# Half-height matmuls of an attention and GEGLU kernel: natural 128-row operands with one exchange of the array halves per unit, and a first chunk in quarters

## The chip, the cores and the metric

The kernel runs on one core of a Trainium2 chip. The metric is the device time of one execution in microseconds (us), median of several runs: 566.61 us before the change (three runs, 566.18 to 568.24). The engines are TensorE (PE, with its weight loads PEld), VectorE (DVE), ScalarE (ACT), GpSimd (POOL) and SyncE (SP, which only issues DMAs here).

## The reference

Shapes: x is [2048, 448]; 16 query heads and 8 key/value heads of 256; only the last 512 keys are attended to; the MLP is 1792 wide. All is bf16.

```
xn = layernorm(x)                                  # no gain, no bias
q  = xn @ wq                                       # [2048, 16*256]
p  = softmax(q @ k[-512:].T / 16)                  # per head, no mask
s  = (p @ v[-512:]) @ wo                           # [2048, 448]
g  = silu((gelu_tanh(xn @ w_gate) * (xn @ w_up)) @ w_down)
out = x + s * g
```

The contraction of the first products is over 448 = 3*128 + 64, which is what this change is about.

## The kernel before, in words

The program is written as a list of operations (`Plan.op`, L69). Each names its engine and the buffers that it reads and writes; `schedule` (L90) turns the dependences into semaphore waits, and `emit` puts each engine's operations out in program order. No engine reorders its list, so the order in the text is the order of the work. Two operations of PE never wait for each other (L80). DMAs are issued from SP, ACT and POOL, each a queue in order.

The 2048 tokens are 16 tiles of 128 and 4 chunks of 512.

- **Layernorm** (L345 to L358). `ln_stats` computes mean and variance of a tile on DVE and 1/sqrt(variance + eps) in two POOL operations (L348, L350). `ln_norm` writes the normalised rows to `xn` on DVE, each group of 64 columns twice, side by side: 896 columns.
- **Transposing** gives `xnT`, with the 448 columns of xn on partitions as 7 blocks of 64, each held twice (partitions 0 to 63 and 64 to 127). The four tiles of chunk 0 go through PE and PSUM (`ln_tp_pe`, L364, copies by ACT and DVE at L380 and L382), the others by DMA on SP's queue (`ln_tp_dma`, L360).
- **The MLP's first products**. A unit is one block of 128 of the 1792 columns, `gu` (L407). Gate weights lie on partitions 0 to 63 and up weights on 64 to 127, 7 blocks of 64 rows each (`load_w`, L316). `pair` (L395) lists 14 matmuls of 64 rows, alternating between the halves of the array, which work at the same time: gate into one PSUM bank, up into the next. A unit uses 2 of the 8 banks, in a ring of four pairs. `gu_evac` (L421) applies gelu on ACT and multiplies by up on DVE, which frees the banks. There are 4 * 14 = 56 units.
- **Chunk 0** starts in halves of 256 tokens for units 0 to 2 (L441 to L458), among the transposes of its four tiles and warm-up matmuls on zeros (`warm`, L386).
- In the main loop (L474) the statistics and the norm of the tiles 4 to 15 alternate with the units, one step per unit from unit 2 on. `down` (L429) multiplies a finished chunk with w_down and stores silu-like gates in `g2`. The loads of wq, v, k, wo are put out at units 27 and 30, those of w_down (`wd`) and of x at the very beginning, on SP's queue (L336 to L342).
- **Attention** (L574 to L594), for each chunk and each group of 8 heads: the queries by `q_pair` (L508), again half-height pairs, head h in one half of the array and head h+4 in the other; then per head scores and exp (`s_mm`), and probabilities times values (`pv`), with the transposing of the result by DMA; the projection with wo of the previous chunk stands between. The end (L595 on) is wo for the last chunk.

Of the kernel before, what the change touches and what calls it, by code (L numbers as in the profile page):

```python
# [11 lines left out]
P = 128  # L12
# [24 lines left out]
class Plan:  # L37
# [31 lines left out]
    def op(self, eng, fn, reads=(), writes=(), dma=False):  # L69
        o = Op(eng, fn, dma)  # L70
        raw = {b.writer: None for b in reads if b.writer is not None}
        deps = dict(raw)
        for b in writes:
            if b.writer is not None:
                deps[b.writer] = None
            deps.update((x, None) for x in b.readers)


        for d in deps:
            if d.eng == eng and not d.dma and not dma and (eng == "pe" or d not in raw):  # L80
                continue
            o.deps.append(d)
        for b in writes:
            b.writer, b.readers = o, []
        for b in reads:
            b.readers.append(o)
        self.ops.append(o)
        return o
# [75 lines left out]
def bass_recurrent_scan__sliding_block_cached__geglu_ffn__prompt_kernel(  # L164
# [25 lines left out]
    NK = D // R  # L190
    att_scale = float(Dh) ** -0.5
    assert D == NK * R and Dh == 256 and W == 512 and Hq == 2 * Hkv and Hq % 8 == 0
    assert NT == 4 * NQC and NF % 2 == 0 and (NQC * NF) % 4 == 0
# [5 lines left out]
    with es:  # L199
# [19 lines left out]

        ident, a_ident, _ = place("ident", [P, P], BF16)  # L220
        b_ident = K.buf(a_ident, 256)
        nhalf, a, _ = place("nhalf", [P, 1], F32)
        b_nhalf = K.buf(a, 4)
        stats, a, _ = place("stats", [P, NT, 6], F32)
# [10 lines left out]
        xnT, a, _ = place("xnT", [P, NK, S], BF16)  # L235
# [8 lines left out]
        wq, a, _ = place("wq", [P, NK, NG, HG // 2, 2, P], BF16)  # L244
        b_wql = [[K.buf() for i in range(2)] for g in range(NG)]
# [13 lines left out]
        NXN = (rw_end - a2) // (2 * D * 2)  # L259
        xn, a, a2 = place("xn", [P, NXN, NK, 2, R], BF16, at=a2)  # L260
        b_xn = sbuf_bufs(a, 2 * D * 2, NXN)
# [3 lines left out]
        wgu, a, at = place("wgu", [P, NK, F], BF16, at=rf)  # L265
        b_wgu = K.buf(a, at - a)
        FBL = [0, 4, 9, NF]
        b_wl = [[K.buf() for j in range(2)] for i in range(3)]
        wd, a, at = place("wd", [P, NF, D], BF16, at=at)
# [3 lines left out]
        NGL = 3  # L273
# [4 lines left out]
        NEX = 2  # L278
# [25 lines left out]
        def mms(lst, reads, writes):  # L304
# [5 lines left out]
            K.op("pe", fn, reads, writes)  # L310
# [5 lines left out]
        def load_w(q, i, j):  # L316
            w = (B_w_gate, B_w_up)[j]
            lo, hi = FBL[i] * P, FBL[i + 1] * P
            dma(q, wgu[R * j:R * j + R, :, lo:hi], w[:, lo:hi].rearrange("(k p) f -> p k f", p=R), (), (b_wl[i][j],))
# [6 lines left out]
        load_w("act", 0, 1)  # L326
        K.op("pool", lambda e: e.memset(ident[:, :], 0.0), (), (b_ident,))
        K.op("pool", lambda e: e.affine_select(
            out=ident[:, :], in_=ident[:, :], compare_op=ALU.not_equal, fill=1.0, base=0,
            pattern=[[-1, P]], channel_multiplier=1), (b_ident,), (b_ident,))  # L330
        K.op("dve", lambda e: e.memset(nhalf[:, :], -0.5), (), (b_nhalf,))
        K.op("dve", lambda e: e.memset(gl[:, 0, :], 0.0), (), (b_gl[0],))
        K.op("dve", lambda e: e.memset(va[:, :, :, Dh:VW], 1.0), (), (b_va1,))

        act(tmp[:, 1, 0:1], nhalf[:, :], ACT.Gelu_apprx_tanh, (b_nhalf,), (b_tmp[1][0],))
        load_w("sp", 1, 0)  # L336
        load_w("sp", 1, 1)
        load_x("sp", 4, 4)
        load_w("sp", 2, 0)
        load_w("sp", 2, 1)  # L340
        load_x("sp", 8, 8)
        dma("sp", wd[:, :, :], B_w_down.rearrange("(f p) d -> p f d", p=P), (), (b_wd,))  # L342


        def ln_stats(t):  # L345
            K.op("dve", lambda e: e.bn_stats(stats[:, t, :], x4[:, t, :]), (b_x4[t],), (b_stats[t],))  # L346
            K.op("dve", lambda e: e.bn_aggr(mv[:, t, :], stats[:, t, :]), (b_stats[t],), (b_mv[t],))  # L347
            K.op("pool", lambda e: e.tensor_scalar(  # L348
# [3 lines left out]

        def ln_norm(t):
            s = t % NXN
            src = x4[:, t, :].rearrange("p (k r) -> p k r", r=R).unsqueeze(2).broadcast_to([P, NK, 2, R])
            K.op("dve", lambda e: e.tensor_scalar(  # L356
                xn[:, s, :, :, :], src, mv[:, t, 0:1], rstd[:, t:t + 1],
                op0=ALU.subtract, op1=ALU.mult), (b_x4[t], b_mv[t], b_rstd[t]), (b_xn[s],))  # L358

        def ln_tp_dma(t):  # L360
            s = t % NXN
            dma_t(xnT[:, :, t * P:(t + 1) * P], xn[:, s, :, :, :].rearrange("p k u r -> p (k u r)"), (b_xn[s],), (b_xnT[t],))

        def ln_tp_pe(t, split):  # L364
            s = t % NXN
            for eng, b, lo, hi in split:
                tp = bank[b].bitcast(BF16)

                def fn(e, tp=tp, lo=lo, hi=hi):
                    ins = None  # L370
                    for k in range(lo, hi):
                        ins = e.transpose(tp[:, k * P:(k + 1) * P], xn[:, s, k, :, :].rearrange("p u r -> p (u r)"), ident[:, :])  # L372
                    return ins
                K.op("pe", fn, (b_xn[s], b_ident), (b_ps[b],))
            for eng, b, lo, hi in split:
                tp = bank[b].bitcast(BF16)
                o = xnT[:, lo:hi, t * P:(t + 1) * P]
                i = tp[:, lo * P:hi * P].rearrange("p (k c) -> p k c", c=P)
                if eng == "act":
                    act(o, i, ACT.Copy, (b_ps[b],), (b_xnTh[t][lo > 0],))  # L380
                else:
                    K.op("dve", lambda e, o=o, i=i: e.tensor_copy(o, i), (b_ps[b],), (b_xnTh[t][lo > 0],))  # L382

        b_xnTh = [[b_xnT[t], K.buf()] for t in range(NT)]
# [10 lines left out]
        def pair(b, w, x, ks, start, stop, lo=0, hi=QC):  # L395
            return [(bank[b + j][:, lo:hi], w(k)[R * j:R * j + R], x(k)[R * j:R * j + R],
                     start and k == ks[0], stop and k == ks[-1]) for k in ks for j in range(2)]
# [4 lines left out]
        def xr_bufs(c, lo=0, hi=4):  # L402
            return [b for t in range(c * 4 + lo, c * 4 + hi) for b in b_xnTh[t]]

        GUB = (0, 2, 6, 4)

        def gu(n, part=None):  # L407
            c, f = divmod(n, NF)
            wi = [i for i in range(3) if FBL[i] <= f][-1]
            b = GUB[n % 4]  # L410
            w = lambda k: wgu[:, k, f * P:(f + 1) * P]
            if part is None:
                lst = pair(b, w, xs(c), range(NK), True, True)
                xb = xr_bufs(c)
            else:
                lo, hi = part * QC // 2, (part + 1) * QC // 2
                lst = pair(b, w, xs(c, lo, hi), range(NK), part == 0, part == 1, lo, hi)
                xb = xr_bufs(c, 2 * part, 2 * part + 2)
            mms(lst, b_wl[wi] + [b_wgu] + xb, (b_ps[b], b_ps[b + 1]))

        def gu_evac(n):  # L421
            c, f = divmod(n, NF)
            s = n % NGL
            b = GUB[n % 4]
# [15 lines left out]

        warm(14, 3)  # L441
        ln_stats(0)
        ln_stats(1)
        ln_norm(0)
        ln_tp_pe(0, [("act", 6, 0, NK)])
        warm(2, 3)
        ln_norm(1)
        ln_tp_pe(1, [("dve", 4, 0, 4), ("act", 5, 4, NK)])
        warm(3, 3)
        ln_stats(2)  # L450
        ln_stats(3)
        gu(0, 0)
        ln_norm(2)
        ln_tp_pe(2, [("dve", 6, 0, 4), ("act", 7, 4, NK)])
        gu(1, 0)
        ln_norm(3)
        ln_tp_pe(3, [("dve", 4, 0, 4), ("act", 5, 4, NK)])
        gu(2, 0)  # L458
# [8 lines left out]
        def load_wq(g, j):  # L467
            lo = (g * HG + j * HG // 2) * Dh
            hi = lo + HG // 2 * Dh
            dma("pool", wq[R * j:R * j + R, :, g, :, :, :].rearrange("p k h e d -> p k (h e d)"),  # L470
                A_wq[:, lo:hi].rearrange("(k p) f -> p k f", p=R), (), (b_wql[g][j],))

        DOWN_AT = {NF + 1: 0, 2 * NF + 3: 1, 3 * NF + 1: 2}
        for n in range(NQC * NF):  # L474
            if n < 3:
                gu(n, 1)
            else:
                gu(n)
            gu_evac(n)
            t = 4 + (n - 2) // 2  # L480
            if n >= 2 and t < NT:
                if n % 2 == 0:
                    ln_stats(t)
                else:
                    ln_norm(t)
                    ln_tp_dma(t)
            if n == 27:
                for g in range(NG):
                    for j in range(2):
                        load_wq(g, j)  # L490
# [4 lines left out]
            if n == 30:  # L495
# [6 lines left out]
            if n in DOWN_AT:  # L502
                down(DOWN_AT[n], 0)

# [3 lines left out]
        def q_pair(c, g, i, b):  # L508

            h, e = divmod(i, 2)  # L510
            mms(pair(b, lambda k: wq[:, k, g, h, e, :], xs(c), range(NK), True, True),
                b_wql[g] + xr_bufs(c), (b_ps[b], b_ps[b + 1]))
            act(qT[:, h, e, :], bank[b], ACT.Copy, (b_ps[b],), (b_qT[h][e],))
            h2 = h + HG // 2
            K.op("dve", lambda v: v.tensor_copy(qT[:, h2, e, :], bank[b + 1]), (b_ps[b + 1],), (b_qT[h2][e],))  # L515
# [57 lines left out]
        bx, by = 0, 4  # L573
        for c in range(NQC):  # L574
            for g in range(NG):
                for i in range(HG):
# [87 lines left out]
```

The softmax here doesn't subtract the row's maximum and nothing guards it: scores larger than these inputs give would overflow.

## Time and profile before

| | |
|---|---|
| median of three runs | 566.61 us (566.18 to 568.24) |
| profiled execution | 567.22 us, its span 565.4 us |
| PE busy in the span | 553.6 us, 98% |
| weight loads | 310.6 us, 55% |
| DVE, ACT, POOL busy | 284.3 us (50%), 209.3 us (37%), 34.5 us (6%) |
| queries, 896 matmuls of 64 rows | 98.1 us |
| MLP's first products with 512 tokens, 742 recorded | 80.9 us |
| first MLP matmul | at 8.96 us |
| norm of one tile on DVE (896 columns) | 0.739 us |
| DMA moved | 42.03 MB |

The span runs from the first to the last instruction of the program; the profiled execution's own time holds a little more on both sides. Busy time of PE is the union of its matmuls' intervals, and those overlap, so a mean of 376 ns for a matmul of 512 columns does not mean that one starts every 376 ns. In a wait "A <- B: sum, times, longest", A stood idle and B's end let it go on. A line number is that of kernel.py; L308 is the helper through which nearly all matmuls go, so groups are told apart by the tiles that they write and read.

### The profile page before, as it was taken

To read this page: it belongs to the slowest core of one execution; us is meant where nothing else is said; L and a number is where in the kernel's file an instruction comes from. 1 tells how busy PE (TensorE), PEld (TensorE's weight loads), DVE (VectorE), ACT (ScalarE), POOL (GpSimd) and SP (SyncE) were. 2 spreads that over 40 slices of the span, in tenths; PEclk is the share of its full clock that TensorE was granted. 3 is DMA by queue.
4 is the path that set the end of the run, shared out by engine and by line. 5 is a ranking of instruction groups with operands and counts; after the bars stand their busy time and mean duration, and the time that the engine had idled before them with its cause. 6 is when DMAs were issued, how large, how long until landed. Compare 5 with 4: busy or idle time off the path is not lost.

```text
span 565.4 us, 9758 instructions
## 1 busy us (share of the span) xinstructions
PE 553.6 (98%) x4037; PEld 310.6 (55%) x4073; DVE 284.3 (50%) x736; ACT 209.3 (37%) x272; POOL 34.5 (6%) x70
## 2 busy tenths in 40 slices
PE   7989999999999999999999999999999999999997
PEld 5534444444466466455655654566465456656656
DVE  5864734244267367314654661267467224665632
ACT  2422423234354554302536531054553303535500
POOL 2111451000000000000000000000000000000000
PEclk9999999999999999999999999999999999999999
DMA  9961599940014124111340430124125011431421
GB/s 205 271 106 23 90 196 243 294 99 1 0 38 84 30 49 84 20 32 37 76 73 18 76 57 17 33 64 84 21 59 84 9 34 48 77 59 30 74 48 34
DMA packets 101708, 42.03 MB, mean 74 GB/s; under 512 B 90464, under 2 KB 98912, under 8 KB 101664
## 3 DMA queue, kind: packets, MB, share of 16 engines
q1 hardware_dynamic: 97648, 29.45, 27.5%
q0 software_dynamic: 3264, 11.27, 8.1%
q10 hardware_dynamic: 752, 0.69, 0.5%
q8 instruction: 32, 0.52, 0.4%
q14 instruction: 12, 0.10, 0.1%
HBM read 17.92 MB, written 1.84 MB: 35 GB/s over the span
## 4 chain that ended last, share of the span: by engine, by line
PE 93%; DVE 3%; issue 1%; DMA 1%; POOL 1%; ACT 0%; DVEq 0%; ACTq 0%
PE bank L308 93%; DVE actT L426 1%; DVE stats L346 1%; POOL rstd L350 1%; DVE xn L356 1%; DMA xnT<-xn 1%; DMA x_65<-in_A_x_dram 0%; PE bank L372 0%; POOL ve L348 0%; DVE mv L347 0%; DVE xnT L382 0%; DVE g_57 L437 0%; ACT gl L302 0%; ACT tmp L302 0%; PE bank L390 0%
## 5 line engine op out<-in xcount | busy, mean ns | idle before, releaser
L302 ACT ACTIVATE expT<-bank 128x1024 bf16<-128x1024 f32 x128 | 123.7, 1022 | 150.6 <-PE bank L308 150.5
L540 DVE TENSOR_SCALAR onorm<-bank,rden 128x256 bf16<-128x256 f32 x256 | 123.8, 484 | 9.6 <-DVE rden L538 0.5
L308 PE MATMUL bank<-va,expT 128*128 128x257 bf16 x1024 | 124.2, 273 | 0.0
L308 PE MATMUL bank<-qT,kT 128*128 128x512 bf16 x476 | 115.9, 379 | 2.9 <-issue 1.3
L308 PEld LDWEIGHTS bank<-va,expT 128*128 128x128 bf16 x1024 | 99.1, 98 | 27.7 <-DVE onorm L540 1.7
L308 PE MATMUL bank<-xnT,wq 64*128 64x512 bf16 x896 | 98.1, 376 | 0.0
L308 PE MATMUL bank<-wo,oT 128*128 128x448 bf16 (+1 forms) x544 | 97.6, 341 | 0.0
L308 PE MATMUL bank<-xnT,wgu 64*128 64x512 bf16 (+1 forms) x826 | 86.0, 366 | 2.4 <-DMA xnT<-xn 2.1
L308 PEld LDWEIGHTS bank<-qT,kT 128*128 128x128 bf16 x512 | 49.1, 97 | 52.3 <-issue 3.4
L308 PEld LDWEIGHTS bank<-wo,oT 128*128 128x128 bf16 x544 | 53.1, 98 | 44.0
L538 DVE RECIPROCAL rden<-bank 128x1 f32<-128x1 f32 x256 | 40.9, 160 | 67.0 <-PE bank L308 67.0
L308 PEld LDWEIGHTS bank<-xnT,wq 64*128 64x128 bf16 x896 | 43.0, 94 | 52.9 <-issue 1.5
L302 ACT ACTIVATE qT<-bank 128x512 bf16<-128x512 f32 x64 | 38.2, 597 | 80.1 <-PE bank L308 80.1
L515 DVE CAST qT<-bank 128x512 bf16<-128x512 f32 x64 | 44.3, 692 | 45.9 <-PE bank L308 45.9
L308 PEld LDWEIGHTS bank<-xnT,wgu 64*128 64x128 bf16 x826 | 39.8, 94 | 47.9 <-DVE actT L426 2.6
L302 ACT ACTIVATE gl<-bank 128x512 bf16<-128x512 f32 x56 | 33.4, 597 | 52.7 <-PE bank L308 48.1
L426 DVE TENSOR_TENSOR actT<-bank,gl 128x512 bf16<-128x512 f32 x56 | 38.5, 687 | 28.5 <-ACT gl L302 28.1
L563 DVE SCALAR_TENSOR_TENSOR tmp<-bank,g_57 128x448 f32<-128x448 f32 (+1 forms) x17 | 10.2, 597 | 82.5 <-PE bank L308 82.5
L308 PE MATMUL bank<-wd,actT 128*128 128x448 bf16 x224 | 43.1, 353 | 0.0
L308 PEld LDWEIGHTS bank<-wd,actT 128*128 128x128 bf16 x224 | 21.7, 98 | 21.2 <-issue 1.3
L296 POOL DMA_DIRECT2D xr<-in_A_x_dram x16 | 8.6, 541 | 379.8 <-DVE ofin L566 375.8
L437 DVE SCALAR_TENSOR_TENSOR g_57<-tmp,bank 128x448 bf16<-128x448 f32 x16 | 9.9, 622 | 33.8 <-ACT tmp L302 33.8
(27 smaller groups left out, 89.3 us busy)
## 6 DMA issues: line engine op xcount, KB each, us to landing
wq<-in_A_wq_dram POOLq DMA_DIRECT2D x4, 896.0 KB, 15.7
wo<-in_A_wo_dram POOLq DMA_DIRECT2D x4, 896.0 KB, 28.0
va<-in_A_v_cache_dram POOLq DMA_DIRECT2D x8, 256.0 KB, 22.8
oT<-onorm SPq DMA_TRANSPOSE x128, 2.5
xr<-in_A_x_dram POOLq DMA_DIRECT2D x16, 112.0 KB, 2.3
out_dram<-ofin SPq DMA_DIRECT2D x15, 112.0 KB, 1.7
wd<-in_B_w_down_dram SPq DMA_DIRECT2D x1, 1568.0 KB, 19.9
wgu<-in_B_w_gate_dram SPq DMA_DIRECT2D x2, 560.0 KB, 11.5
```

Source lines behind the costliest of these rows:

```text
L296: K.op(q, lambda e, o=o, i=i: e.dma_start(o, i), reads, writes, dma=True)
L302: K.op("act", lambda e, o=o, i=i: e.activation(o, i, func, scale=scale), reads, writes)
L308: ins = e.matmul(o, lhsT=l, rhs=r, start=st, stop=sp)
L346: K.op("dve", lambda e: e.bn_stats(stats[:, t, :], x4[:, t, :]), (b_x4[t],), (b_stats[t],))
L350: K.op("pool", lambda e: e.tensor_tensor(rstd[:, t:t + 1], ve[:, t:t + 1], nhalf[:, :], ALU.pow), (b_ve[t], b_nhalf), (b_rstd[t],))
L356: K.op("dve", lambda e: e.tensor_scalar(xn[:, s, :, :, :], src, mv[:, t, 0:1], rstd[:, t:t + 1], op0=ALU.subtract, op1=ALU.mult), (b_x4[t] ...
L426: K.op("dve", lambda e: e.tensor_tensor(actT[:, c % 2, f, :], bank[b + 1], gl[:, s, :], ALU.mult), (b_ps[b + 1], b_gl[s]), (b_actT[c % 2][ ...
L437: K.op("dve", lambda e, t=t, b=b, s=s: e.scalar_tensor_tensor(out=g2[:, t, :], in0=tmp[:, s, :], scalar=1.0, in1=bank[b][:, 0:D], op0=ALU. ...
L515: K.op("dve", lambda v: v.tensor_copy(qT[:, h2, e, :], bank[b + 1]), (b_ps[b + 1],), (b_qT[h2][e],))
L538: K.op("dve", lambda e, bb=bb, r=r: e.reciprocal(rden[:, r:r + 1], bank[bb][:, Dh:Dh + 1]), (b_ps[bb],), (b_rden[r],))
L540: K.op("dve", lambda e, bb=bb, r=r, t4=t4: e.tensor_scalar(onorm[:, o, t4, h % 2, :], bank[bb][:, 0:Dh], rden[:, r:r + 1], None, op0=ALU.m ...
L563: K.op("dve", lambda e: e.scalar_tensor_tensor(out=tmp[:, s, c0:c1], in0=bank[b][:, c0:c1], scalar=0.5, in1=g2[:, t, c0:c1], op0=ALU.mult, ...
```

## The change

What it does:

1. **Layout.** xn's 448 columns are laid out as 3 blocks of 128 and one of 64; only the last 64 are held twice. `xnT` has 4 blocks instead of 7, xn 512 columns instead of 896, now written by two DVE instructions. The weights lie as 3 blocks of 128 rows in `wgu` and `wq`, with the remaining 64 rows in `wgur` and `wqr`: gate's (or the first half of a head) on partitions 0 to 63, up's (or the second half) on 64 to 127. Packets in the loads have other sizes: columns 0 to 2, 2 to 6 and 6 to 14 of the units instead of 0 to 4, 4 to 9, 9 to 14.
2. **Order of the matmuls.** `group` takes two units (4 banks) at a time. First phase: for unit A and then B, the remainder and the three blocks, gate from rows 0 to 63 and up from rows 64 to 127. Second phase: the three blocks with the halves exchanged, so that every bank gets the other half of its rows. Since a bank is now written from both halves of the array, the second phase of a unit waits for the end of its first (`after`, a wait of PE for itself). Queries go the same way with the two halves of one head's 256 columns in place of gate and up, two heads to a group.
3. **The first chunk.** Only units 0 and 1 are done in parts, in quarters of 128 tokens, one after each tile's transposing. The root for tiles 0 to 3 is taken by ACT (Sqrt) and DVE (reciprocal) instead of POOL; ACT's table of Gelu is loaded after that. There are 20 warm-up matmuls ahead of it instead of 14, 2 and 3.
4. **Loads.** x of the tiles 8 to 11 and 12 to 15 and w_down go to POOL's queue, behind units 4, 8 and 6; the loads of wq, v, k, wo all follow the last tile's norm.
5. **Buffers.** gl has 4 instead of 3, expT 3 instead of 2.

The core of the diff:

```diff
-    def op(self, eng, fn, reads=(), writes=(), dma=False):
+    def op(self, eng, fn, reads=(), writes=(), dma=False, after=()):
...
+        o.deps.extend(after)
...
-        xnT, a, _ = place("xnT", [P, NK, S], BF16)
+        xnT, a, _ = place("xnT", [P, NK + 1, S], BF16)
...
-        wgu, a, at = place("wgu", [P, NK, F], BF16, at=rf)
+        wgu, a, at = place("wgu", [P, 2, NK, F], BF16, at=rf)
+        wgur, _, at = place("wgur", [P, F], BF16, at=at)
-        FBL = [0, 4, 9, NF]
+        FBL = [0, 2, 6, NF]
...
-            dma(q, wgu[R * j:R * j + R, :, lo:hi], w[:, lo:hi].rearrange("(k p) f -> p k f", p=R), (), (b_wl[i][j],))
+            dma(q, wgu[:, j, :, lo:hi], w[0:K3, lo:hi].rearrange("(k p) f -> p k f", p=P), (), (b_wl[i][j],))
+
+        def load_wr(q, i, j):
+            w = (B_w_gate, B_w_up)[j]
+            lo, hi = (0, FBL[1] * P) if i == 0 else (FBL[1] * P, F)
+            dma(q, wgur[R * j:R * j + R, lo:hi], w[K3:D, lo:hi], (), (b_wlr[i][j],))
...
-        load_x("sp", 8, 8)
-        dma("sp", wd[:, :, :], B_w_down.rearrange("(f p) d -> p f d", p=P), (), (b_wd,))
...
+        def ln_std_act(t):
+            K.op("act", lambda e: e.activation(ve[:, t:t + 1], mv[:, t, 1:2], ACT.Sqrt, bias=epst[:, :]),
+                 (b_mv[t], b_epst), (b_ve[t],))
+
+        def ln_recip(t):
+            K.op("dve", lambda e: e.reciprocal(rstd[:, t:t + 1], ve[:, t:t + 1]), (b_ve[t],), (b_rstd[t],))
...
-            src = x4[:, t, :].rearrange("p (k r) -> p k r", r=R).unsqueeze(2).broadcast_to([P, NK, 2, R])
+            for lo, hi, src in ((0, D, 0), (D, DP, K3)):
...
-        def pair(b, w, x, ks, start, stop, lo=0, hi=QC):
-            return [(bank[b + j][:, lo:hi], w(k)[R * j:R * j + R], x(k)[R * j:R * j + R],
-                     start and k == ks[0], stop and k == ks[-1]) for k in ks for j in range(2)]
+        last_row = {}
+
+        def group(units, x, lo, hi, start, stop, reads):
+            for ph in range(2):
+                for i, (b, w, wr) in enumerate(units):
+                    lst = []
+                    for k in ([NK] if ph == 0 else []) + list(range(NK)):
+                        for u, j in ((0, ph), (1, 1 - ph)):
+                            rows = slice(R * u, R * u + R)
+                            l = wr[rows] if k == NK else w(j, k)[rows]
+                            lst.append((bank[b + j][:, lo:hi], l, x(k)[rows], start and k == NK,
+                                        stop and ph == 1 and k == NK - 1))
+                    o = mms(lst, reads, b_ps[b:b + 2], [last_row[b]] if b in last_row else [])
+                    last_row[b] = o
...
-        warm(14, 3)
-        ln_stats(0)
-        ln_stats(1)
-        ln_norm(0)
-        ln_tp_pe(0, [("act", 6, 0, NK)])
-        warm(2, 3)
...
+        warm(20, 3)
+        ln_first(0)
+        ln_first(1)
+        ln_second(0)
+        ln_second(1)
+        ln_tp_pe(0, 4, "act")
+        ln_stats(2)
+        ln_std_act(2)
+        ln_tp_pe(1, 5, "dve")
+        gu_group(0, 0, 0)
+        gu_group(0, 0, 1)
+        ln_second(2)
+        ln_first(3)
+        ln_tp_pe(2, 6, "act")
+        gu_group(0, 0, 2)
+        ln_second(3)
+        ln_tp_pe(3, 7, "dve")
+
+        act(tmp[:, 1, 0:1], nhalf[:, :], ACT.Gelu_apprx_tanh, (b_nhalf,), (b_tmp[1][0],))
+        gu_group(0, 0, 3)
...
+        for n in range(0, NQC * NF, 2):
+            if n > 0:
+                gu_group(n, cur)
+            gu_evac(n, cur)
+            if n > 0:
+                ln_step()
+            gu_evac(n + 1, cur + 2)
+            if n > 0:
+                ln_step()
+            cur = 4 - cur
+            if n == 4:
+                load_x("pool", 8, 4)
+            if n == 6:
+                dma("pool", wd[:, :, :], B_w_down.rearrange("(f p) d -> p f d", p=P), (), (b_wd,))
+            if n == 8:
+                load_x("pool", 12, 4)
...
+        def q_group(c, h, b):
+            units = [(b + 2 * i, lambda j, k, i=i: wq[:, k, (h + i) * Dh + j * P:(h + i) * Dh + (j + 1) * P],
+                      wqr[:, h + i, :]) for i in range(2)]
+            group(units, xs(c), 0, QC, True, True, b_wql[h // HG] + b_xnT[c * 4:c * 4 + 4])
```

Here `ln_first` is the statistics and ACT's root, `ln_second` the reciprocal and the norm, and `ln_step` the next of statistics (with POOL's root) or norm and DMA transposing, for tiles 4 to 15. `gu_group(n, b, part)` calls `group` for units n and n+1 on the banks b to b+3, with `part` on 128 of the 512 tokens.

## The prediction

> **What bounds the kernel now.** I read the page first: busy shares, the 40 slices and the groups.
>
> ```profile
> PE 553.6 (98%) x4037; PEld 310.6 (55%) x4073; DVE 284.3 (50%) x736; ACT 209.3 (37%) x272; POOL 34.5 (6%) x70
> ...
> PE   7989999999999999999999999999999999999997
> ...
> L308 PE MATMUL bank<-xnT,wq 64*128 64x512 bf16 x896 | 98.1, 376 | 0.0
> ```
>
> TensorE is the bound: 98% busy, with nearly all its idle time in the first three slices and the last. The last line is the form that the change reorders: 896 half-height matmuls in 98.1 us are 448 pairs of 0.219 us, two halves of the array at once. Then the windows by stage, which place the 11.8 us in which PE does nothing (columns: length, then busy time of PE, PEld, DVE, ACT, POOL with counts, granted clock, DMA share, GB/s).
>
> ```profile
> 0.00:12.80 12.80, 8.93 (x77) 6.20 (x79) 7.12 (x18) 3.38 (x5) 3.82 (x14) 1.00 0.90 202
> 12.80:32.50 19.70, 19.70 (x211) 10.08 (x210) 15.08 (x28) 8.25 (x14) 3.96 (x10) 1.00 1.15 244
> 32.50:34.80 2.30, 0.21 (x4) 0.12 (x4) 2.05 (x5) 0.60 (x1) 0.64 (x2) 1.00 1.16 178
> 34.80:130.00 95.20, 95.20 (x752) 44.25 (x753) 43.81 (x71) 31.01 (x53) 19.64 (x33) 1.00 0.66 145
> 130.00:562.50 432.50, 429.58 (x3004) 249.96 (x3036) 215.48 (x615) 166.09 (x199) 6.47 (x12) 1.00 0.25 47
> ```
>
> Two places are open: the start (idle, warm-up matmuls and transposes), and a hole at 32.5, where chunk 1 should begin. The waits and the chain name that hole's cause; the DMA issues say why it exists.
>
> ```profile
> PE bank L308 <- DMA xnT<-xn: 2.1, 1, 2.1
> ```
> ```profile
> 30.74 0.46 DVE actT L426
> 31.20 3.42 DMA xnT<-xn
> 34.71 108.14 PE bank L308 x868
> ```
> ```profile
> xnT<-xn SPq DMA_TRANSPOSE x12, 3.4
> oT<-onorm SPq DMA_TRANSPOSE x128, 2.5
> wd<-in_B_w_down_dram SPq DMA_DIRECT2D x1, 1568.0 KB, 19.9
> ```
>
> wd is issued at 10.78 on SP's queue and lands 19.9 later, at 30.7. The four transposes of chunk 1 sit behind it in that queue: the first, issued at 20.03, lands at 31.47, the fourth at 34.62, though its norm ended at 29.48. With an empty queue a transpose takes 2.9 (the minimum).
>
> **The change, part by part.** Sums are against the profiled execution, 567.22 us (span 565.4 and 1.8 around it), 0.6 above the median of 566.61.
>
> Steady matmuls: nothing removed. A unit is still 14 half-height matmuls, 7 pairs (0.216 apart, a unit every 1.511); each pair still fills both halves into two banks. Only the order differs: 4 pairs of unit A, 4 of B, then A's other 3 with the halves exchanged, B's 3.
>
> New are two waits of PE on itself per group: A's second part waits for the end of A's first. There are 28 groups in the MLP, one of them in quarters, and 32 for the queries: 59 full groups, 118 waits. Queued behind each are the next pairs' weight loads on PE, and behind those every evacuation. The trace has no such wait, so bounds. A 512-column matmul ends 0.376 after its start and a landed release was followed by PE 0.09 later (34.62 to 34.71): 0.47 after A's last start. The order puts 0.216 and B's 4 pairs (0.864) between: 1.08. For B's wait A's 3 pairs leave 0.86. Cover left 0.4 to 0.6 us, so 0; waits already met now cost PE nothing (units stay 1.511 apart). Without cover, each costs from 0.05 (a semaphore instruction on PE) to 0.16 (the largest "issue" step at a change between array forms): 6 to 19 us. A gain is excluded, as no matmul goes. I take 0.
>
> Evacuation: two units now come together every 3.02 us. A's tanh-gelu 0.60 and product 0.69, B's the same; the other four banks cover 3.02, and DVE needs 1.4 plus LN. LN on DVE is stats 0.62, aggregate 0.18, norm; today a step of that loop takes 3.16 (norms at 19.26 and 22.42), more than PE's 3.02. B's banks are wanted again 3.9 after its end, so this costs nothing while DVE stays under that. Third expT and fourth gl buffer: PE is not waiting there today, 0.
>
> Norm: 896 elements in 0.739 become 448 and 64. DVE's plain pace is 1.04 ns an element (448 in 0.625, 224 in 0.392), so onorm's 256 in 0.484 leave 0.217 fixed, and norm's own row 0.58 ns per element: 0.48 + 0.25, less 0.08 of overlap between DVE instructions: 0.65. Bounds 0.5 and 0.96 (one element per cycle).
>
> The start, walked. x tile 0 lands at 3.25; both statistics end at 4.85. The root moves from POOL (0.22 + 0.57) to ACT (nearest row: 128x1 ACTIVATE, 0.20), done by 4.5 behind the stats, then reciprocal (at most the 0.16 of a PSUM one): norm 0 from 5.06 to 5.7. The 20 warm-up matmuls at today's 0.226 (14 in 3.17) end at 5.7 and take nothing from it. Transposes: 4 instead of 7. Here the trace shows two paces:
>
> ```profile
> 5.93 0.93 PE L372 MATMUL bank<-ident,xn 128*128 128x128 bf16 x7 [1.55 <-DVE xn L356]
> ...
> 12.28 0.56 PE L372 MATMUL bank<-ident,xn 128*128 128x128 bf16 x7
> ```
>
> That is 0.11 apiece early and 0.056 later, although the clock column says 1.00. So 0.6 for the first four, to 6.35; ACT copies 512 columns in 0.60 (384 take 0.491, 896 take 0.917): first quarter at 7.0, against 8.96 for the first half today. Weights are there: the first block, 448 KB a matrix, lands at 8.7 today; two units are half of that, and 2.5 after an issue near 3.4 is 6. The next (1024-byte rows) needs 12.9; the trace's 1024-byte packets take 46 ns, the 1280-byte ones now in its place 110.
>
> A quarter is 14 pairs of 128 columns. Lower bound 0.056 a pair, 0.8; upper 0.11, 1.55, and 0.25 of self-waits too short to be covered (a 128-column matmul ends after 0.22, B's 4 pairs last 0.22). I take 1.0, near the later transposes. Quarters 0 and 1: 7.0 to 9.0. Tile 2's transposes to 9.4; its copy on ACT stands behind the root of tile 3, to 10.1. Quarter 2 to 11.1, transposes 11.45, DVE copy (0.425) 11.9, quarter 3 to 12.9. Two units done then; today three are at 15.84, so two at 14.33. **Gain 1.4.** With 0.8 a quarter it is 1.9; with 1.8 for the first two, -0.1; for all four, -1.7.
>
> The Trainium skill, "TensorE: Matmul & The Clock Gate", Part 1, says that the clock is halved until about 3.4 us of sustained activity fill a free-running window. The two paces agree with it. By the rule 20 warm-ups (4.5 us) may open the clock before 7.0 or miss it by their phase: gain 1.9 or -0.1.
>
> ACT now loads a Sqrt table (1.28, as today's first, under the x load) and then, after tile 2's copy, the Gelu table: 10.1 + 1.28 + 0.2 = 11.6, before the first gelu at 12.8. Nothing; even 1 us late, the third group uses other banks. "ScalarE: Activation LUTs", What ACT_TABLE_LOAD costs, speaks against this: a change of set takes about 2.66 us with its drain. By it the first gelu starts at 13.0, 0.2 late, still not on PE's path. Here today's load was followed by its ACTIVATE after 0.01, but with an empty pipe.
>
> The hole. wd, x 8 to 11 and 12 to 15 go to POOL's queue, issued there after the rstd of tiles 5, 6, 7 (about 0.75, 1.5 and 0.75 of POOL, from wo's 0.886 for 1024 rows, within 3 us of slack each). So no transpose stands behind wd. From the end of the group in which tile 7 has its turn: product A ends 0.9 later, statistics 1.7, product B 2.4, POOL's rstd 2.65, norm 3.3, and the transpose (2.5, oT's row has the same 128x512) lands at 5.8; chunk 1 comes at 6.05. The margin is 0.25, and wd's packets (1792 of 46 ns on 16 queues, 5.2 us) run beside it; the halved load frees the engines otherwise. I leave 0.3 of today's 2.2 (0 to 1.0). **Gain 1.9.** x 8 to 11 is wanted about 31, some 8 after its issue. wd: issued about 24.7, lands about 32.5, needed at 34. Later loads (wq, v, wo from unit 24 on) are wanted only from 130 on. The end does not change.
>
> Sum: -1.4 - 1.9 = -3.3: 563.9 for the profiled execution, **563.3** against the median.
>
> **The rivals.** (1) The start gives nothing: quarters at the slow pace, or copies and transposes in series eat it. For: quarters load weights for 128 columns only, and tiles 2 and 3 leave PE idle 0.5 to 0.8 each. Against: the pace of 0.056. 566.6 - 1.9 + 0.1 to 1.0 = 564.8 to 565.7. (2) Slower: PE's wait on itself at each exchange. If the sequencer cannot run ahead over it, PE runs dry 118 times; for it, no row shows PE waiting for PE; against it, 0.4 us of cover. At 0.05 each 563.3 + 5.9 = 569.2, at 0.16 582. From 0.028 each the kernel is slower than before. (3) wd or tile 7 is late through POOL's queue: 1 to 2 us back, 564.3 to 565.3. (4) Everything fits: start 1.9, hole 2.2 and some: below 562.5.
>
> **How the numbers follow.** Forecast case (562.2 to 564.6) 0.56; rival 1 0.16; rival 2 0.14; rival 3 0.06; rival 4 0.08. About 0.5%, 2.8 us, is what a measurement of this kernel can tell from no change. Below 563.8 lie two thirds of the forecast case (0.37) and rival 4: 0.45. Within: 0.19 + 0.16 + 0.06 = 0.41. Slower 0.14. The range 562.0 to 566.8 takes in both gains at their bounds except four slow quarters, and leaves out rival 2 and half of rival 4.
>
> **What would show it.** Right: units of chunk 0 from about 13 on; no PE wait for xnT near 31, transposes landing within 3 us of their norms; query groups of 3.02 us as now; no PE wait on PE in the list. Wrong: gaps between parts of a group, pairs over 0.11 in the quarters, a wait for wd before the first down, or ACT_TABLE_LOAD more than 3 times.

## The result, and the profile after

The changed kernel takes 571.94 us (four runs, 571.32 to 572.68) against 566.39 for the kernel before: a ratio of 1.0093, interval 1.0066 to 1.012. It is slower by about 5 us; 563.3 was forecast. The profiled execution took 571.32 us, its span 569.3, 3.9 more than before.

The stages, in the windows that were shown of the kernel before (length, busy time of PE, PEld, DVE, ACT, POOL, granted clock, DMA share, GB/s):

```profile
0.00:12.80 12.80, 10.08 (x146) 7.13 (x148) 6.93 (x26) 5.34 (x10) 0.68 (x6) 1.00 0.84 225
12.80:32.50 19.70, 18.44 (x176) 9.49 (x172) 14.97 (x34) 8.22 (x14) 6.90 (x13) 1.00 0.62 188
32.50:34.80 2.30, 0.00 (x0) 0.00 (x0) 1.50 (x5) 0.00 (x0) 0.79 (x2) 0.88 1.20 236
34.80:130.00 95.20, 92.92 (x712) 43.25 (x714) 39.22 (x74) 29.08 (x50) 20.66 (x34) 0.97 0.57 139
130.00:562.50 432.50, 429.68 (x3005) 248.38 (x3038) 215.38 (x615) 168.05 (x202) 6.46 (x12) 1.00 0.25 47
```

The start is denser than it was (10.08 of 12.8 against 8.93). The last stage, with all the attention, is the same (429.68 against 429.58). The hole at 32.5 is not closed but wider: PE does nothing in the whole third window, and loses time in the windows on both sides of it. The clock column is below 1.00 there, which it was nowhere before. The waits and the chain name the hole:

```profile
PE bank L317 <- DMA xnT<-xn: 5.8, 1, 5.8
```
```profile
28.37 0.17 DVE actT L456
28.54 8.46 DMA xnT<-xn
36.99 0.09 issue
37.08 110.09 PE bank L317 x868
```

Tile 7's transpose is put out at 28.5, a microsecond earlier than the norm of the same tile ended in the kernel before, and lands at 36.99. Three windows around the hole show what follows it:

```profile
31.00:37.10 6.10, 0.25 (x6) 0.05 (x3) 3.00 (x8) 0.87 (x2) 0.79 (x2) 0.77 1.19 219
37.10:41.10 4.00, 4.00 (x20) 1.69 (x22) 0.00 (x0) 0.00 (x0) 0.00 (x0) 0.50 0.05 9
41.10:60.00 18.90, 18.90 (x133) 8.95 (x130) 8.42 (x18) 5.75 (x10) 1.58 (x4) 1.00 0.04 9
```

The clock is 0.50 for the first 4.0 us of chunk 1: 20 recorded matmuls start in them, where 37 would at full pace.

**The ledger**, from the two traces. Two units are done at 12.93 instead of 14.33: -1.4. From the place where the next pair would have followed chunk 0's last unit to chunk 1 are 6.0 (31.07 to 37.08) instead of 2.2 (32.50 to 34.71): +3.8. (The wait rows give a little less, 5.8 and 2.1, since the last matmul was still running.) Chunk 1's first two units, up to the first matmul of down, take 5.08 instead of 3.13: +1.95, the slow clock. From there to the first query it is 92.76 in both. What is left, to the end, is 0.4 shorter. Sum +3.95; the spans differ by 3.9. The medians differ by more, 5.5, since the profiled execution of the kernel before was among its slower and that of the changed kernel its fastest.

What held the transpose is in the DMA view of 20 to 37 us, by queue (packets, MB, share of 16 engines), and in the issues below it:

```profile
q0 software_dynamic: 640, 2.52, 49.6%
q1 hardware_dynamic: 2975, 0.72, 34.9%
...
wd<-in_B_w_down_dram POOLq DMA_DIRECT2D x1, 1568.0 KB, 9.3
x_67<-in_A_x_dram POOLq DMA_DIRECT2D x2, 448.0 KB, 6.6
xnT<-xn SPq DMA_TRANSPOSE x6, 5.0
```

POOL's queue moved its 2.52 MB in 640 packets, almost 4 KB each: most packets of the trace are 4480 bytes, five rows of 896, and take about 200 ns. A transpose of 128x512 is 512 packets of 256 bytes and 18 ns, 32 for each of the 16 engines. Tile 6's transpose was put out at 25.90, tile 7's behind it at 28.54. From 27 to 31 us the DMA view shows:

```profile
q0 software_dynamic: 259, 1.16, 92.6%
q1 hardware_dynamic: 45, 0.01, 1.4%
```

So 259 packets of POOL's queue passed and 45 of the transposes'. Tile 6's transpose landed at 36.78, 10.9 us after it was put out, and tile 7's at 36.99; the last of POOL's loads landed at 36.42. The Trainium skill says in "DMA: Bandwidth & Descriptors", Queues, rings and completion order, that a DMA engine goes round the queues that have work and takes a whole packet from one before it switches. These counts do not show such turns one for one; why so few of the small packets passed stays open.

### The profile page after: what moved, and what is told of

It is laid out like the page before. It is cut to its first block, busy times and chain, and to the rows that moved or that the text cites. A ratio compares the mean times of both kernels' runs of the same rounds, so it can differ in the third digit from the quotient of the medians.

```text
span 569.3 us, 9817 instructions
## 1 busy us (share of the span) xinstructions
PE 555.1 (98%) x4068; PEld 312.0 (55%) x4104; DVE 279.6 (49%) x756; ACT 210.7 (37%) x276; POOL 35.5 (6%) x67
## 4 chain that ended last, share of the span: by engine, by line
PE 93%; DVE 3%; DMA 2%; issue 1%; POOL 1%; ACT 0%; DVEq 0%
PE bank L317 93%; DMA xnT<-xn 1%; DVE stats L363 1%; DVE xn L382 1%; DVE actT L456 1%; DMA x_67<-in_A_x_dram 0%; POOL rstd L369 0%; DVE mv L364 0%; POOL ve L367 0%; DVE xnT L405 0%; DVE g_58 L467 0%; ACT xnT L311 0%; ACT gl L311 0%; ACT tmp L311 0%; DVE tmp L625 0%
## 5 line engine op out<-in xcount | busy, mean ns | idle before, releaser
L317 PE MATMUL bank<-xnT,wq 64*128 64x512 bf16 x768 | 93.3, 376 | 0.0
L317 PE MATMUL bank<-xnT,wgu 64*128 64x512 bf16 (+1 forms) x744 | 84.5, 361 | 0.0
L576 DVE CAST qT<-bank 128x512 bf16<-128x512 f32 x64 | 42.9, 692 | 47.1 <-PE bank L317 47.1
L317 PEld LDWEIGHTS bank<-xnT,wq 64*128 64x128 bf16 x768 | 37.4, 94 | 44.7
L317 PEld LDWEIGHTS bank<-xnT,wgu 64*128 64x128 bf16 x744 | 36.5, 95 | 37.9 <-issue 2.0
L456 DVE TENSOR_TENSOR actT<-bank,gl 128x512 bf16<-128x512 f32 x56 | 37.3, 685 | 37.3 <-ACT gl L311 23.4
L311 ACT ACTIVATE gl<-bank 128x512 bf16<-128x512 f32 x56 | 33.2, 597 | 58.8 <-PE bank L317 58.2
L625 DVE SCALAR_TENSOR_TENSOR tmp<-bank,g_58 128x448 f32<-128x448 f32 (+1 forms) x17 | 10.2, 597 | 82.5 <-PE bank L317 82.5
L317 PE MATMUL bank<-xnT,wgur 64*128 64x512 bf16 (+1 forms) x124 | 23.0, 364 | 7.1 <-DMA xnT<-xn 5.8
```

The costliest lines, as they stand in the source:

```text
L311: K.op("act", lambda e, o=o, i=i: e.activation(o, i, func, scale=scale), reads, writes)
L317: ins = e.matmul(o, lhsT=l, rhs=r, start=st, stop=sp)
L456: K.op("dve", lambda e: e.tensor_tensor(actT[:, c % 2, f, :], bank[b + 1], gl[:, s, :], ALU.mult), (b_ps[b + 1], b_gl[s]), (b_actT[c % 2][ ...
L576: K.op("dve", lambda v, h8=h8, bb=bb: v.tensor_copy(qT[:, h8, 1, :], bank[bb + 1]), (b_ps[bb + 1],), (b_qT[h8][1],))
L625: K.op("dve", lambda e: e.scalar_tensor_tensor(out=tmp[:, s, c0:c1], in0=bank[b][:, c0:c1], scalar=0.5, in1=g2[:, t, c0:c1], op0=ALU.mult, ...
```

## The experiments

Theory A: POOL's large packets starve SP's transposes, chunk 1 waits, and the idle time halves the clock. Theory B: the layout or the new order costs, and the late transposes are late by themselves or for another reason.

The kernel before, measured beside each group of experiments, had a median of 567.88 us with e1 to e4 and of 566.91 with the others, against 566.39 with the changed kernel. Differences to the changed kernel are differences of medians and good to about 1 us; a ratio is always to the kernel before of the same group.

**e1: the loads undone.** x of the tiles 8 to 15 and w_down go back to SP's queue at the start.

```diff
         load_w("sp", 2, 1)
+        load_x("sp", 8, 8)
+        dma("sp", wd[:, :, :], B_w_down.rearrange("(f p) d -> p f d", p=P), (), (b_wd,))
...
-            if n == 4:
-                load_x("pool", 8, 4)
-            if n == 6:
-                dma("pool", wd[:, :, :], B_w_down.rearrange("(f p) d -> p f d", p=P), (), (b_wd,))
-            if n == 8:
-                load_x("pool", 12, 4)
```

> The changed kernel with one part undone: x of the tiles 8 to 15 and w_down are issued on SP's queue at the start again, behind the MLP weights, and POOL issues none of them. Theory A (POOL's queue moves packets of 4480 bytes, 173 to 204 ns each, on the same 16 DMA engines, and each 256-byte packet of a transpose has to wait for one of them, so that tile 7's transpose takes 8.5 us, PE stands idle 5.9 us, and the clock is halved until 41.1): the weights land at 18.0, then x and w_down need 7.8 us by the packets of the kernel before, to about 26; tile 7 lands about 31; the idle 5.9 and the 2.0 of the slow clock go: 571.9 - 7.9 + 0 to 0.5 = 564.0 to 564.5, 2 us faster than before. Theory B (the transposes of 512 columns are late by themselves, or the order of the matmuls costs): 570 to 572, a wait for xnT near 31 stays.

Measured: 563.45 us, ratio to the kernel before 0.9929 (0.9913 to 0.9944). Windows of e1:

```profile
12.80:31.00 18.20, 18.11 (x168) 8.15 (x170) 13.53 (x31) 6.86 (x13) 3.95 (x10) 1.00 1.03 241
31.00:33.00 2.00, 2.00 (x22) 0.93 (x22) 1.97 (x6) 0.84 (x2) 0.11 (x1) 1.00 0.16 31
33.00:130.00 97.00, 97.00 (x770) 45.18 (x768) 43.80 (x82) 33.47 (x57) 21.49 (x36) 1.00 0.55 135
```

The hole is gone, the clock stays at 1.00. w_down lands at 26.15 and tile 7's transpose at 30.88, just before chunk 1 at 31.04. Layout, order, waits and quarters are all in this kernel: together with the start they are worth about 4 us, and the moved loads cost 8.5 (9.3 by the ratios).

w_down stands ahead of the transposes in SP's queue here as it did in the kernel before, and the hole is gone all the same, because everything ahead of them lands earlier: the last gate and up weights at 18.0 instead of 22.95, w_down at 26.15 instead of 30.72. The 1792 packets of 1280 bytes and about 110 ns of the kernel before do not occur in the new layout. That they are the whole reason was not tried by itself.

**e2: the loads alone**, in the kernel before (the same three loads from POOL, behind the units 5, 7 and 9).

> The kernel before with that one part alone: x of the tiles 8 to 11, w_down and x of 12 to 15 go to POOL's queue behind the units 5, 7 and 9; layout, order and start are the old ones. Theory A: the transposes of chunk 1 have 896 columns, nearly twice the packets, and pass only when POOL's queue is empty, about 36.5: PE waits from 32.5 to 38 or 39 instead of to 34.7 and then has 2 us of slow clock: 570 to 573. Theory B: SP's queue is rid of w_down, the wait of 2.2 us shrinks: 564 to 566.

Measured: 577.88 us, ratio 1.0165 (1.0125 to 1.0206); single runs from 572.4 on. The waits and one window of e2:

```profile
PE bank L308 <- DMA xnT<-xn: 8.7, 1, 8.7
```
```profile
43.30:48.20 4.90, 4.85 (x24) 2.10 (x26) 0.88 (x2) 0.60 (x1) 0.00 (x0) 0.50 0.24 53
```

Here the loads alone slow the kernel, by more than I had said: the hole ends at 43.3, and the clock is halved for longer, 10.2 us (38.0 to 48.2). Theory B falls. That part of the profiled execution's loss lies in its start, where the clock was halved too (7.3 to 14.1), is one reason for the size; the fastest run, 572.4 with a mean clock of 0.994 against 0.985 in the profiled one, lies where I had put it. The transposes of tiles 6 and 7 landed at 42.63 and 43.26, POOL's last load at 42.46. From 38 to 42 us only 37 packets of POOL's queue passed and 638 of SP's, so large packets in front of small ones are not the whole account of this wait.

**e3: the hole filled** with matmuls on old data, ahead of the first group of chunk 1.

```diff
+            if n == NF:
+                fill(56, cur)
```

`fill` puts out 56 matmuls of 256 columns into a bank that is overwritten afterwards.

> The changed kernel with 56 matmuls of 256 columns on old data (their results are overwritten) put ahead of chunk 1's first group, 6.0 us of work in the 5.9 us of idle time. If the halved clock after the hole is an own cost of 2.0 us: 571.9 - 2.0 + 0.1 = 570.0, the granted clock 1.00 from 34.8 on, chunk 1 still not before 37.0. If the clock has nothing to do with it: 572.0.

Measured: 569.66 us, ratio 1.004 (1.0024 to 1.0056). Windows of e3:

```profile
31.00:39.20 8.20, 6.43 (x58) 5.39 (x56) 2.97 (x8) 0.84 (x2) 0.79 (x2) 1.00 1.37 163
39.20:44.00 4.80, 4.74 (x37) 2.39 (x38) 1.36 (x4) 1.18 (x2) 0.00 (x0) 1.00 0.06 10
```

Chunk 1 does not come earlier (39.2 in this execution, its slowest run), but the clock is 1.00 after the hole. The median is 2.3 us less than the changed kernel's (3.0 by the ratios, whose intervals do not meet): the slow clock is a cost of its own, as the ledger has it.

**e4: the wait without its cover.** The two phases of a unit directly one after the other.

```diff
-            for ph in range(2):
-                for i, (b, w, wr) in enumerate(units):
+            for i, (b, w, wr) in enumerate(units):
+                for ph in range(2):
```

> The changed kernel with the two phases of each unit directly one after the other (A first, A second, B first, B second), so that nothing stands between PE's wait on itself and what it waits for. If the wait costs what its cover lacks: 0.376 + 0.09 - 0.216 = 0.25 us for each of the 118, 29 us: 601; query groups 3.5 us apart instead of 3.02. If such waits cost nothing at all, cover or not: 572.

Measured: 599.43 us, ratio 1.0562 (1.0531 to 1.0593), 27.5 us over the changed kernel: 0.233 for each of 118 waits (0.225 by the ratios). From e4's waits, where the 126 are the 118 and 8 in the quarters and the 68.4 us are idle time of the weight loads, not of the matmuls; then from its timeline:

```profile
PEld bank L317 <- PE bank L317: 68.4, 126, 1.0
```
```profile
21.24 0.38 PE L317 MATMUL bank<-xnT,wgur 64*128 64x512 bf16 x2
21.24 0.53 PEld L317 LDWEIGHTS bank<-xnT,wgu 64*128 64x128 bf16 x6
...
22.33 0.33 PEld L317 LDWEIGHTS bank<-xnT,wgu 64*128 64x128 bf16 x6 [0.56 <-PE bank L317]
22.99 0.38 PE L317 MATMUL bank<-xnT,wgur 64*128 64x512 bf16 x2
```

Units come 1.75 apart (21.24, 22.99) instead of 1.51. In the changed kernel no line with PE waiting for PE is among the waits, and the eight query blocks take 12.42 each, as before. So the price is real and the second unit between the phases hides all of it.

**e5: POOL's loads earlier**, all three behind unit 2.

> The changed kernel with all three loads still on POOL's queue, but put out together behind unit 2 (about 19 to 22) instead of behind the units 4, 6 and 8. Theory A says that what counts is whether POOL's packets run beside a transpose that chunk 1 needs: they take 7.8 us of the DMA engines, from about 21 to 29 or 30, so tile 5's and 6's transposes land about 30 and tile 7's, put out at 28.5, about 31: the hole shrinks from 5.9 to 0 to 0.5 and the slow clock goes: 564.0 to 564.7. If POOL's queue is a harm wherever it stands, or the late transposes have another cause: 569 to 572.

Measured: 565.65 us, ratio 0.9975 (0.9964 to 0.9986). The wait in e5:

```profile
PE bank L317 <- DMA xnT<-xn: 1.8, 1, 1.8
```

The hole shrinks from 5.8 to 1.8 and the clock stays up, so it is not POOL's queue as such but the overlap of its loads with the transposes that costs. I was 1 us too low: the last of the loads landed at 31.6, not at 29 or 30, and tiles 5, 6 and 7 all landed between 31.9 and 32.9, right behind it.

**e6: the same loads from ACT's queue**, at the same places.

> The changed kernel with the same three loads at the same places, issued from ACT's queue, whose packets were 896 bytes and 41 to 46 ns in the trace, instead of POOL's with 4480 bytes and 173 to 204 ns. If the size of the other queue's packet sets the price of a turn (theory A): a transpose has some 32 packets for each of the 16 engines, 32 times 46 + 18 ns is 2.0 us instead of 7, so tile 7 lands at 31 to 32 and the hole is 0 to 1 us: 564.0 to 565.5. If any load beside the transposes starves them: a hole of 4 us or more and a slow clock, 570 to 572. ACT's own time for the three issues, 0.6 to 1.3 us each, has the slack of the other four banks.

Measured: 567.56 us, ratio 1.0001 (0.9988 to 1.0014). The DMA view of e6 from 27 to 31 us:

```profile
q10 hardware_dynamic: 1213, 1.07, 91.8%
q1 hardware_dynamic: 715, 0.17, 21.9%
```

The loads' 2.52 MB are 2864 packets here, most of them of 896 bytes. Beside 1213 packets of ACT's queue 715 of the transposes' passed in these four microseconds, against 45 beside 259 in the changed kernel, with about as many bytes moved by the other queue. The turns are not one for one here either, which stays unexplained. The hole is 2.2 us by the wait rows instead of 5.8:

```profile
31.00:33.20 2.20, 0.05 (x2) 0.00 (x0) 2.17 (x6) 0.68 (x2) 0.38 (x2) 1.00 1.08 156
33.20:38.00 4.80, 4.76 (x28) 2.00 (x28) 0.96 (x4) 0.60 (x1) 0.41 (x1) 0.64 0.16 32
```

I had said 0 to 1. And the smaller hole does not show that the size of the packets sets the price, for the loads also ran earlier. ACT put them out at 19.0, 22.0 and 25.1; POOL, where they stand behind a tile's root, at 21.6, 24.6 and 27.7. The last of them landed at 32.7 instead of 36.4, 3.7 us earlier, and chunk 1 came 3.8 us earlier. If the end moves with the issue, 2.6 of these come from the earlier issue, and little more than 1 us is left for the size of the packets or the kind of the queue, which e6 does not tell apart.

2.2 us of idle time were enough to halve the clock for 3.4 us (34.5 to 38.0) in this execution. The ten runs lie at 565.8 to 566.3 (three) and 567.3 to 568.8 (seven); their mean granted clock, which is on record for each run, is 1.0 in the three and 0.997 in the seven, so it happened in these and not in those.

**e7: only w_down on POOL's queue.**

> The changed kernel with only w_down on POOL's queue, behind unit 6 as in the change; x of the tiles 8 to 15 goes behind the MLP weights on SP at the start. Theory A: w_down alone holds tile 6's and tile 7's transposes back until it has landed. In the changed kernel 1.6 MB with 0.46 MB of x behind it kept the queue busy from about 27.5 to 36.4; w_down alone should be done near 32.5, both transposes near 33.3: a hole of about 2.0 us in place of 5.9, 565.5 to 566.5, with the slow clock or without it up to 568. If the x loads on POOL are what holds them: no hole, 563.5. If neither: 570 to 572.

Measured: 568.27 us, ratio 1.0016 (1.0001 to 1.0031). From the waits, then the windows, of e7:

```profile
PE bank L317 <- DMA xnT<-xn: 3.2, 1, 3.2
```
```profile
34.20:40.10 5.90, 5.90 (x28) 2.25 (x28) 0.25 (x2) 0.60 (x1) 0.00 (x0) 0.50 0.13 25
```

w_down alone holds tiles 6 and 7 until it has landed (33.2; they follow at 33.60 and 34.11). The hole is 3.2, not 2.0, in part since w_down landed 0.7 later than I had put it; with the slow clock, the time lies a little over what I gave. Two of the ten runs have a mean clock of 1.0 and take 566.9 and 567.1; six at 0.997 take 567.95 to 569.3, two at 0.994 take 569.6. That is the price of the slow clock again, within one kernel.

**e8: a trim of the start**, on top of e1: tile 2's transposes ahead of quarter 1, the remainder rows in three loads.

```diff
...
         gu_group(0, 0, 0)
+        ln_second(2)
+        ln_tp_pe(2, 6, "act")
+        ln_first(3)
         gu_group(0, 0, 1)
-        ln_second(2)
-        ln_first(3)
-        ln_tp_pe(2, 6, "act")
...
```

> The kernel of e1 (loads on SP), and beyond it: tile 2's norm and transposes ahead of quarter 1, its copy ahead of tile 3's root on ACT, and the remainder rows loaded in three blocks, so that those of the units 2 to 5 come before x of the tiles 4 to 7. From e1's trace: quarter 2 at 9.1 instead of 9.55, quarter 3 at 10.9 instead of 11.4, and no wait of 0.44 for the remainder rows at 12.9: 0.5 to 0.9 us less than e1, 562.5 to 563.0. If tile 3's root, now later, decides: 563.4, no change from e1.

Measured: 562.93 us, ratio 0.9923 (0.9909 to 0.9937), the fastest of all. The first full group in e1 and in e8:

```profile
12.89 0.39 PE L317 MATMUL bank<-xnT,wgur 64*128 64x512 bf16 x2 [0.44 <-DMA wgur<-in_B_w_up_dram]
```
```profile
12.28 0.39 PE L317 MATMUL bank<-xnT,wgur 64*128 64x512 bf16 x2
```

In the profiles 0.6 us earlier, in the medians 0.5. The intervals of e1's and e8's ratios overlap, and they were not run side by side, so the gain over e1 is likely and not shown.

**e9 and e10: why the kernel before spreads.** Its runs range from 565.7 to 569.6, e1's only from 563.3 to 563.7. e9 has 21 warm-up matmuls instead of 14, e10 fills the old wait of 2.1 us with 20 matmuls on old data.

> The kernel before with 21 warm-up matmuls in place of 14, so that PE does not stand idle from 4.4 to 5.9. If the spread of the kernel before (566.0 to 568.8 in the runs so far) comes from the moment at which the clock is granted at the start: runs within 0.6 us of each other, median 565.5 to 566.5, 1 to 2 us under the unchanged kernel of the same chip. If the clock at the start has no part in it: the same spread and median as before, 567 to 568.

> The kernel before with 20 matmuls of 256 columns on old data (their results are overwritten) ahead of chunk 1's first unit, 2.1 us of work in its wait of 2.1 us. If the spread of the kernel before (565.9 to 568.9) comes from this hole, which in some executions halves the clock for a window as the hole of 2.2 us in e6 did: runs within 0.8 us of each other, 565.9 to 566.6, no time of 567.5 or more. If the hole has no part in the spread: times up to 568.5 as before.

Measured: e9 566.74 us, ratio 0.9997 (0.9985 to 1.0009), runs from 566.07 to 568.83. e10 568.44 us, ratio 1.0012 (0.9995 to 1.0028), runs from 566.77 to 569.99. The spread stays in both, so neither the warm-up nor the hole alone explains it. The mean clock of the single runs does not sort them either: the kernel before has a run of 566.4 at 0.993 and one of 569.0 at 1.0. It stays open. In four profiles with the old layout the first weights land at 8.7, 8.8, 9.3 and 10.1, and the first MLP matmul follows at 9.0, 9.1, 9.6 and 10.4; with the new layout they are there at 6.4 to 7.1. That would fit, but was not tried by itself.

## Why the prediction was wrong

- **Start: right, mechanism and size.** Two units at 12.93; 12.9 was forecast. The quarters took 0.96 (1.0 forecast), tile 2's copy stood where it was put, and the norm took 0.61, forecast 0.65. The Gelu table was loaded by 11.4 and hindered nobody: the change of set took 1.28 (10.11 to 11.40), not the 2.66 that was weighed beside it. One term was off and cost nothing by luck: the first weights landed at 7.05, not at 6, and the first quarter's other operand was ready at 7.08.
- **Waits of PE on itself: right.** No cost in the changed kernel. The price without cover, 0.05 to 0.16 in the prediction, was too low; e4 gives 0.233, near the 0.25 by which the 0.47 of a matmul's tail and release exceeds the 0.216 to the next pair. Rival 2 had the sign of the result, but not its cause.
- **The hole: wrong, and this is the step that failed**: "wd's packets (1792 of 46 ns on 16 queues, 5.2 us) run beside it", hence "I leave 0.3 of today's 2.2 (0 to 1.0)". The overlap of POOL's loads with the transposes was taken as nearly free. Up to there the walk was right: tile 7's transpose was put out at 28.54 and with its 2.5 us would have landed at 31.04, when PE was ready for it. It landed at 36.99, after 8.46, and the hole became 6.0 where 0.3 was left for it. What the runs show in place of the step: without the overlap there is no hole (e1), with less of it the hole is smaller (e5, e7), the loads alone make it in the kernel before (e2), and in every profile with loads on a second queue tile 7's transpose lands behind the last of them. The 46 ns are a row of SP's queue; from POOL's queue the same rows travel five to a packet, about 200 ns each. How much of the delay the size of the packets makes is not shown. The mechanism was written down as rival 3 and priced at 1 to 2 us, without a row for POOL's queue. Yet the page of the kernel before had one, in its part on the queues:

```profile
q1 hardware_dynamic: 97648, 29.45, 27.5%
q0 software_dynamic: 3264, 11.27, 8.1%
```

11.27 MB in 3264 packets are 3.5 KB each, and 8.1% of 16 engines over 565.4 us are 0.22 us for each, against 25 ns for a packet of q1. If each of a transpose's 32 packets on an engine had to let one of these pass, that alone would be 7.2 us. That sum could have been made as a warning. That it comes near the 8.5 measured is luck: two transposes stood in the queue, and the packets did not pass one for one.
- **A term that was missing: the clock.** The hole was priced as idle time alone. Behind it 4.0 us ran at half pace, 2.0 lost; e3 takes 2.3 off by filling the hole. The prediction weighed the clock for the start and did not ask about it for the hole.
- **Put together**, the forecast of 563.3 is close to the time of this change without its moved loads: e1 takes 563.45. That is luck in part: the 1.9 for the hole were to come from the moved loads, and in e1 they come without them, from weights that land 5 us earlier. The prediction had the faster packets of the new layout at hand and used them for the start alone.
- **A loose reading** that bears on no term: of the 11.8 us in which PE did nothing, 2.9 lie between 130 and 562.5, not at the two ends.

## What to carry to other kernels

When a load is moved to another queue to get out of a transfer's way, it still shares the DMA engines with it. Here a transpose of many small packets, put out beside loads of another queue, landed only when these had landed. So ask when the loads will have landed, by bytes and by packets of their own queue (bytes and share over packets, from the page), and keep the urgent transfer clear of them in time, not just in another queue. First see whether the loads ahead of it can land earlier: in e1, where the weights landed 5 us earlier, the hole was gone without a second queue. An idle gap of PE of two microseconds or more can be paid twice, once as idle time and once as slow clock behind it; and a wait of PE on its own result is free as long as other matmuls, here 0.65 us or more of them, stand between.

## What the runs showed of the hardware that was not expected

- A transpose put out beside loads of another queue waited for them: tile 7's landed 0.4 to 1.3 us behind the last of these loads in six profiles (36.42 and 36.99 in the changed kernel, 31.64 and 32.89 in e5, 33.20 and 34.11 in e7), 1.8 in e3.
- Loads of 896-byte rows were packets of mostly 4480 bytes and about 0.2 us from POOL's queue, and of 896 bytes and 41 to 55 ns (medians) from SP's and ACT's.
- The clock was halved for 3.4 (e6), 6.8 (the changed kernel, e4, e7) or 10.2 us (e2), beginning in or behind holes of 2.2 us (e6), 3.2 (e7), 4.6 (e4), 5.8 and 8.7 (e2), and not with one of 1.8 (e5). The hole of 2.1 in the kernel before left it at 1.00, and in three of e6's ten runs the mean clock is 1.0, so near 2 us the length alone does not decide. In e6 it fell 1.3 us after PE had resumed.
- Packets of 1280 bytes into 64 partitions took about 110 ns (12 bytes a ns); those of 1024 bytes, in the same layout and also into 64 partitions, 46 (22 bytes a ns). In the new layout 512, 1024 and 2048 bytes took 27, 46 and 87 ns (19 to 24 bytes a ns), 3072 bytes into 64 partitions 150 to 200. Why those of 1280 were slow stays open.
